# Attention scores by half blocks of 160 columns, six transfers a head pair, and the product with the global values by 64 rows

## The chip, the cores and the metric

The program runs on one core of one Trainium2 chip. The metric is the device time of one execution in microseconds. Before the change it is 891.88 us, the median of 3 runs (891.61 to 892.87).

## The reference

Attention feeds two feed-forward layers. There are 4 batches of 8 heads, 512 local tokens, 32 global tokens and 64 values a head. A global token looks at all 544 keys; a local one looks at the 32 global keys and at the local keys at most 32 places away.

```python
s_g = scale * np.matmul(q_g, k_all.transpose(0, 1, 3, 2))      # 32 x 544
out_g = np.matmul(sm(s_g), v_all)
mask = np.abs(pos[:, None] - pos[None, :]) <= 32
s_ll = np.where(mask, scale * np.matmul(q_l, k_l.transpose(0, 1, 3, 2)), -1e9)
s_lg = scale * np.matmul(q_l, k_g.transpose(0, 1, 3, 2))
a_l = sm(np.concatenate([s_lg, s_ll], axis=-1))
out_l = np.matmul(a_l, np.concatenate([v_g, v_l], axis=2))
x = concatenate([out_g, out_l]) as 2176 tokens x 512
x = (silu(x @ w_gate) * (x @ w_val)) @ w_out                   # d_ff 1536
h = x @ w_in;  out = (h * tanh(softplus(h))) @ w_out           # d_ff 2048
```

All inputs are float32, the feed-forward weights float64.

## The kernel before, in words

**Two parts.** The first is attention (`attention`, L537) for 16 head pairs, n = 0 to 15, four to a batch. With it run the conversion of the first six weight tiles and, as filling, two tiles (512 and 384 tokens) of the first feed-forward group (`add_fill`, L640). The second part is the rest of both feed-forward layers, placed by a planner (`run`, L1323) that works from its own costs and due times and is untouched by the change.

**The order of the attention part** is written out: `ORDER` (L221) is a string with a letter for each task, `KINDS` (L218) says what each letter is and on which of its two possible engines it runs, and `in_order` (L242) walks it and hands out PSUM banks. There are two double banks, `PAIR`, and four single ones, `ONE`; a task that needs a bank takes the next free one and holds it until a named task has read it. Each engine works through its own tasks in that order, and so does SP's queue with its transfers. After the first 18 TensorE tasks `attention` puts in as many products of zeros (`keep_busy`, L155) as the digits of `steady` (L550) say, 19 in all, and `setup` puts in 7.

**A head pair** (`add_pair`, L265) goes through these tasks:

- `qk`, SP: `load_qk` (L172) has two transfers for k (L178) and four for q (L180 to L183), the last rows of q together with the first ones. For pair 0 the q transfers are on ACT's queue. `v`, SP: `load_v` (L195) has four, windows of 128 keys that start every 64 keys (L202 to L204).
- `A`, TensorE: 16 transposes of k and q by 64 rows (L212, tiles `ks`, `qs`) into a double bank. `Ak`, `Aq`, DVE or ACT: copies to SBUF (L237 or L235, `kst`, `qT`).
- `Ag`, `At`, POOL: the global keys and the overlapping 64 keys of the next block are copied into `kst` (L287, L293, L294), so that each of the four blocks of 128 queries has 192 local and 32 global keys side by side.
- `S`, TensorE (L314), one for each half g: for 2 blocks and 2 heads a product of 64 rows (a head's values) and 128 output lines (queries) with 224 columns, into a double bank, a head to a bank.
- `M`, DVE (L325): mask and row minimum of 224 columns, one instruction for each block and head. `E`, ACT (L332): exponential with its sum. `R`, DVE: reciprocal. `N`, POOL or DVE (L344, L346): product with the reciprocal, 4 x 192 and 4 x 32 columns.
- `C`, TensorE (L212, `sm`, `sng`): 10 transposes of the weights into a double bank. `V`: copied to SBUF (`pt`).
- `D`, TensorE (`values`, L374): first 8 products with the global values (L378; 128 rows, of which `vg` has zeros in all but 32, 64 output lines, 128 columns), then 16 with the local ones (L382; 128 rows, 64 output lines, 64 columns), all into one single bank. `Xc`: copied out; `Xh`, `Xl`: split into two parts; `Xd`: stored.

**The global queries** go two head pairs at a time (`add_glob`, L398): `GA` (L408) 2 products of 512 columns, `GM`, `GE`, `GR`, `GN` as above, `GT` 10 transposes (tile `sg`), `GO` (L454) 20 products of 32 columns. `add_batch` (L472) turns the global keys and queries (L478).

**Float32 products** are recorded as two instructions each, transposes as one: the 4 products of an `S` task show as 8.

Of the kernel before, what the change touches and what calls it, by code (L numbers as in the profile page):

```python
# [21 lines left out]
def tile_attn_moe_moe2(  # L22
# [57 lines left out]
    kst_p = pool("kst", 2, early)  # L80
# [11 lines left out]
    mask = e_p.tile([128, 224], F32, name="mask")  # L92
    mask7 = e_p.tile([128, 224], F32, name="mask7")
    qgbd = e_p.tile([128, HP, 2, SG], F32, name="qgbd")
    vg = e_p.tile([128, 4, HP, D], F32, name="vg")
    vgb = e_p.tile([128, H, D], F32, name="vgb")

    def setup():
        nc.gpsimd.memset(ident, 1.0)
        nc.gpsimd.affine_select(out=ident, in_=ident, pattern=[[-1, 128]], compare_op=ALU.is_equal,  # L100
                                fill=0.0, base=0, channel_multiplier=1)
        keep_busy(0, 7)
        nc.vector.memset(qgbd, 0.0)
        for t in (vg, vgb):
            nc.vector.memset(t, 0.0)

        nc.gpsimd.memset(mask, 0.0)
        m = mask[:, 0:192]
        nc.gpsimd.affine_select(out=m, in_=m, pattern=[[1, 192]], compare_op=ALU.is_ge,
                                fill=NEG, base=0, channel_multiplier=-1)  # L110
        nc.gpsimd.affine_select(out=m, in_=m, pattern=[[-1, 192]], compare_op=ALU.is_ge,
                                fill=NEG, base=64, channel_multiplier=1)

        nc.gpsimd.tensor_copy(mask7, mask)
        nc.gpsimd.memset(mask7[64:96, 128:192], NEG)
        nc.gpsimd.memset(mask7[96:128, 64:128], NEG)
# [4 lines left out]
    def x_copy(src, key, cols, name):  # L121
        XF[key] = sm_p.tile([128, 512], F32, tag="xf", name="xf")[:, 0:cols]
        duplicate(name, XF[key], src)
# [26 lines left out]
    QS, KS, VW, KST, GK = {}, {}, {}, {}, {}  # L150
# [21 lines left out]
    def load_qk(b, hp):  # L172
# [6 lines left out]
        for h in range(2):  # L179
            eng.dma_start(out=qs[:, 0:3, h],  # L180
                          in_=q_l[b, 2 * hp + h, SG:SG + 384, :].rearrange("(c p) d -> p c d", p=128))
        eng.dma_start(out=qs[0:96, 3], in_=q_l[b, hs, SG + 384:SL, :].rearrange("h p d -> p h d"))
        eng.dma_start(out=qs[96:128, 3], in_=q_l[b, hs, 0:SG, :].rearrange("h p d -> p h d"))  # L183
        QS[b, hp], KS[b, hp] = qs, ks

    def load_vg(b):

        for k in range(4):
            nc.sync.dma_start(out=vg[32 * k:32 * k + 32, k],
                              in_=v_g[b].rearrange("(g h) p d -> h p g d", h=2)[k % 2])  # L190

    def load_vgb(b):
        nc.sync.dma_start(out=vgb[96:128], in_=v_g[b].rearrange("h p d -> p h d"))

    def load_v(b, hp):  # L195

        hs = slice(2 * hp, 2 * hp + 2)
        vw = v_p.tile([128, NB, 2, D], F32, tag="vw", name="vw")
        for h in range(2):
            v = v_l[b, 2 * hp + h]  # L200
            windows = bass.AP(v.tensor, v.offset, [[D, 128], [64 * D, NB - 1], [1, D]])
            nc.sync.dma_start(out=vw[:, 0:NB - 1, h], in_=windows)  # L202
        nc.sync.dma_start(out=vw[0:64, NB - 1], in_=v_l[b, hs, SL - 64:SL, :].rearrange("h p d -> p h d"))
        nc.sync.dma_start(out=vw[64:128, NB - 1], in_=v_l[b, hs, 0:64, :].rearrange("h p d -> p h d"))  # L204
# [5 lines left out]
    def transpose_half(out, src, j):  # L210
# [7 lines left out]
    KINDS = ("qk A gk w Ak+1 Aq At Cq AG AGk Ag S M E AGe GG GA GGe+1 Cf GM R vg v vgb N Ak GE GR GN C V "  # L218
             "Ch GT GV D AGk+1 Aq+1 GO Xc GXc+1 Xd GV+1 Cl Xc+1 GXh+1 Xh Xh+1 Xl GXl V+1 Ch+1 GXd F_v "
             "F_g GXc Ft Fg Fp Fh Fl Fh+1 GXl+1 F2 Fy Fy+1 GXh Xl+1").split()  # L220
    ORDER = "abcdaefgchaijkllmkmmmmmmnnnnibopedcnqgnramsnntbskfelfhluvammmmmmmmwnxnnngyybizgsAnBCkfDEDEnqsslmmFnnGcHm"  # L221
    ORDER += "muwnntlbnIemnnJAyayKmmmigDEDoBslkCEalpLkmmmmmnMnnumnGnnnmNmnnnIyywOwPbaQRDznESfOqDlsuyETUlmmmmmmmmnnnnyI"
    ORDER += "DDnrnnEngVVkWdtLXbwAlMefIusYZcmvOlmmQmgnUnnBbmmmM01ayymzhsnnf2DDnEEnCdqlssscgVGwnIUHamnmlummMVtnSAnyWyk1"
    ORDER += "YmmmmnnnnnUb0zxKOZaDXQiiDBlEjhul3Immm4kCyg1mmmmmVb5nnnnnnnnDsLefyEGwuoRTHl6DqEpy2lmOnmnmymnSgsbekkrfImmm"
    ORDER += "nnmDZwOadaE7nWns1tsYcDlgLEQVlmmAmmbInnnnu3eRmmyyqkmmKlUnn2D0wvVRBnEtDC4mmm00USWgVncm5GnuEhnnlOwy1s8xiHbd"
    ORDER += "7msmmyAnIefaDnnsmEn13nBCilsnMDjou0LyyEmmmml4wOGnnnngphmmmZkPrIDmw5Dnnnn0uEEbUlYssImeOMOmmmfUn2SqskyyVaDD"
    ORDER += "sZaELgEtlFQQlMImnnVkmmmm9TAnmBmmbVCnM2nnn!!xzufnnn#ylb!y!emmnnnSm#n6Km#gkwvwDDXX17gnZlOOddulmm$UIqWyymmm"
    ORDER += "mmmtGD1nnnnnnnnEu0P3ADVl45EL6lwIwmmnmnnmnyyBmmm7mNZnnnnDCuD!My!OREyXUGI%DU9PDEL$#X&VI2%9OMTOMUZ!!$$O&&"
# [36 lines left out]
    def add_pair(n):  # L265
# [15 lines left out]
        def kst():  # L281
            if (b, hp) not in KST:
                KST[b, hp] = kst_p.tile([128, 4, 224], F32, tag="kst", name="kst")
            return KST[b, hp]

        def glob_keys():
            nc.gpsimd.tensor_copy(kst()[:, :, 192:224], GK[b, "kT"][:, hp:hp + 1, :].to_broadcast([128, 4, SG]))  # L287

        def keys():
            duplicate(("Ak", n), kst()[:, :, 0:128].rearrange("c r (j t) -> c r j t", j=2), R["pk"])  # L290

        def more_keys():
# [1148 lines left out]
```

## Time and profile before

| | us |
|---|---|
| median of 3 runs | 891.88 |
| the profiled execution | 890.72 |
| its span, first to last instruction | 889.0 |
| attention part, to the last of its products | 159.0 |
| TensorE busy | 877.6 |
| DVE, ACT, POOL busy | 649.6, 490.8, 541.3 |

The granted TensorE clock is at full speed throughout the span. Busy time counts every moment at which an instruction of the engine is under way, its tail included, so a TensorE that is busy isn't one that starts instructions as fast as it can. Transfers have no busy time of their own on the queue that issues them; the queue's timeline shows how long each issue takes.

### The profile page before, as it was taken

How to read it: one execution, taken by the hardware profiler on the slowest of the kernel's cores; microseconds unless marked ns; L12 is line 12 of the kernel's file. 1: busy time of each engine (PE TensorE's matmuls, PEld its weight loads, DVE VectorE, ACT ScalarE, POOL GpSimd, SP SyncE). 2: the span in 40 equal slices, each digit the busy share in tenths (PEclk: the TensorE clock that was granted, in tenths of full speed). 3: DMA queues.
4: the chain of work that ended last, by engine and by line, in shares of the span. 5: the costliest groups of instructions: out<-in, count | busy, mean ns of one | idle time of the engine just before them, and what ended most of it. 6: DMA issues, size and time to landing. Idle time of an engine off the chain costs nothing.

```text
span 889.0 us, 17205 instructions
## 1 busy us (share of the span) xinstructions
PE 877.6 (99%) x6252; PEld 808.0 (91%) x6252; DVE 649.6 (73%) x1224; ACT 490.8 (55%) x1177; POOL 541.3 (61%) x550
## 2 busy tenths in 40 slices
PE   7999999999999999999999999999999999999998
PEld 6777888988999999999999999998989898989896
DVE  5777786779777888778778899777777777753434
ACT  6888886454435454455455678764445444544341
POOL 4798887699964386375374799564454436633231
PEclk9999999999999999999999999999999999999999
DMA  7777775577555646646546335664737374726283
GB/s 167 169 182 168 189 173 147 197 233 240 195 190 197 224 148 209 205 139 230 178 153 221 137 142 194 224 222 156 250 116 261 121 263 139 259 80 197 61 266 144
DMA packets 165334, 164.19 MB, mean 185 GB/s; under 512 B 81793, under 2 KB 143745, under 8 KB 165249
## 3 DMA queue, kind: packets, MB, share of 16 engines
q1 hardware_dynamic: 163824, 162.24, 57.8%
q8 instruction: 49, 0.80, 0.4%
q10 hardware_dynamic: 1424, 0.85, 0.3%
q14 instruction: 37, 0.30, 0.1%
HBM read 136.31 MB, written 26.74 MB: 183 GB/s over the span
## 4 chain that ended last, share of the span: by engine, by line
PE 94%; DMA 2%; SPq 1%; DVE 1%; ACT 0%; issue 0%; ACTq 0%; DVEq 0%
PE p L1127 37%; PE p L1232 21%; PE p L1018 15%; PE p L1084 8%; PE one L650 3%; PE pair L212 2%; PE pair L314 2%; PE one L378 1%; PE one L382 1%; DMA qs<-in_q_l 1%; PE one L454 1%; DMA gkq<-in_q_g 1%; PE one L408 1%; DMA vw<-in_v_l 0%; SPq L178 0%
## 5 line engine op out<-in xcount | busy, mean ns | idle before, releaser
L1127 PE MATMUL p<-xh,w 128*128 128x384 f32 (+1 forms) x992 | 258.3, 326 | 0.0
L1232 PE MATMUL p<-w,a 128*128 128x512 f32 x816 | 194.3, 391 | 0.0
L1232 PEld LDWEIGHTS p<-w,a 128*128 128x128 f32 x816 | 152.2, 188 | 29.9
L1127 PEld LDWEIGHTS p<-xh,w 128*128 128x128 f32 x992 | 176.9, 188 | 1.4
L1127 PE MATMUL p<-xl,w 128*128 128x384 f32 (+1 forms) x496 | 161.5, 326 | 0.0
L1139 ACT ACTIVATE b<-p 128x384 f32<-128x384 f32 (+1 forms) x144 | 68.0, 472 | 158.1 <-PE p L1127 153.7
L1018 PE MATMUL p<-a,w 128*128 128x384 f32 (+2 forms) x768 | 142.8, 334 | 0.0
L1048 POOL TENSOR_TENSOR a<-b,a 128x384 fp32r<-128x384 f32 (+1 forms) x58 | 62.0, 1068 | 117.9 <-ACT a L1046 76.6
L1018 PEld LDWEIGHTS p<-a,w 128*128 128x128 f32 x768 | 130.5, 188 | 2.8
L1242 DVE TENSOR_TENSOR y<-p,y 128x512 f32<-128x512 f32 x119 | 82.1, 690 | 65.3 <-PE p L1232 63.8
L880 POOL TENSOR_TENSOR w<-cx,w 128x256 fp32r<-128x256 f32 (+1 forms) x90 | 100.0, 1119 | 44.4 <-ACT w L879 38.9
L833 DVE TENSOR_TENSOR b<-p,b 128x384 f32<-128x384 f32 (+1 forms) x144 | 76.3, 531 | 64.2 <-PE p L1127 42.9
L1048 POOL TENSOR_TENSOR a<-s,a 128x384 fp32r<-128x384 f32 (+2 forms) x53 | 61.5, 1161 | 65.8 <-ACT a L1046 65.8
L1127 PE MATMUL p<-e,w 128*128 128x384 f32 (+1 forms) x528 | 101.3, 328 | 0.0
L1127 PEld LDWEIGHTS p<-xl,w 128*128 128x128 f32 x496 | 93.1, 188 | 1.5
L1127 PEld LDWEIGHTS p<-e,w 128*128 128x128 f32 x528 | 90.0, 188 | 1.0
L1027 DVE TENSOR_TENSOR y<-p,y 128x384 f32<-128x384 f32 (+2 forms) x116 | 62.5, 542 | 22.7 <-PE p L1018 21.3
L1084 PE MATMUL p<-xh,w 128*128 128x384 f32 (+1 forms) x256 | 72.6, 355 | 0.0
L1046 ACT ACTIVATE a<-s 128x384 fp32r<-128x384 f32 (+2 forms) x88 | 45.4, 516 | 47.0 <-DVE s L1070 45.9
L591 DVE SCALAR_TENSOR_TENSOR fl<-q,st 128x512 f32<-128x512 f32 x68 | 62.4, 918 | 9.8 <-ACT q L583 9.6
L595 DVE SCALAR_TENSOR_TENSOR cx<-fl,cx 128x512 uint32<-128x512 uint32 x68 | 65.9, 969 | 0.5
L332 ACT ACTIVATE sm<-sm,nb 128x224 f32<-128x224 f32 x128 | 60.0, 473 | 3.7 <-DVE nb L325 3.6
(153 smaller groups left out, 1512.9 us busy)
## 6 DMA issues: line engine op xcount, KB each, us to landing
e<-td SPq DMA_DIRECT2D x76, 384.0 KB
xh<-td SPq DMA_DIRECT2D x38, 384.0 KB
xl<-td SPq DMA_DIRECT2D x38, 384.0 KB
st<-in_moe_w_out SPq DMA_DIRECT2D x28, 512.0 KB
st<-in_moe_w_in SPq DMA_DIRECT2D x16, 512.0 KB
vw<-in_v_l SPq DMA_DIRECT2D x32, 224.0 KB
e<-td SPq DMA_DIRECT2D x20, 320.0 KB
st<-in_moe_w_gate SPq DMA_DIRECT2D x12, 512.0 KB
```

The costliest lines, as they stand in the source:

```text
L591: nc.vector.scalar_tensor_tensor(fl, q, TINY2, hw, op0=ALU.is_ge, op1=ALU.mult)
L595: nc.vector.scalar_tensor_tensor(x, fu, 0xC0000000, x, op0=ALU.bitwise_and, op1=ALU.bitwise_or)
L833: return lambda e: vec(e).tensor_tensor(out=out(), in0=a(), in1=b(), op=op)
L880: add(lo or [("POOL", PO(n))], 0, lambda e: vec(e).tensor_tensor(out=dst(1), in0=src(), in1=dst(0).bitcast(F32), op=ALU.subtract), r=[rd, ...
L1018: nc.tensor.matmul(ps.h[:, 0:n], lhsT=a.h[:, d], rhs=b.h[:, at:at + n], start=(i == 0 and j == 0), stop=(i == len(ws) - 1 and j == 2))
L1027: add("DVE", DV(n), lambda e: nc.vector.tensor_tensor(out=ya, in0=ps.h[:, 0:n], in1=ya, op=ALU.add), r=[ps], w=yt)
L1048: t.append(add(either(n), 0, lambda e: vec(e).tensor_tensor(out=dst(1), in0=get(), in1=dst(0).bitcast(F32), op=ALU.subtract), r=[v, (av[0] ...
L1084: nc.tensor.matmul(ps.h[:, 0:n], lhsT=a.h[:, d], rhs=b[:, c, c0:c0 + n], start=(c == 0 and j == 0), stop=(c == KD - 1 and j == 2))
L1127: nc.tensor.matmul(ps.h[:, 0:n], lhsT=w.h[:, 256 * a + 128 * c:256 * a + 128 * c + 128], rhs=xs[b][:, c, :], start=(start and c == 0 and j ...
L1139: add("ACT", AC(n), lambda e: nc.scalar.activation(out=dst.h[:, 0:n], in_=src.h[:, 0:n], func=AF.Copy), r=[sv], w=[dst])
L1232: nc.tensor.matmul(ps.h, lhsT=a.h[:, d], rhs=b.h, start=(i == 0 and q == 0), stop=(i == len(ws) - 1 and q == 2))
L1242: add("DVE", DV(512), lambda e: nc.vector.tensor_tensor(out=ya, in0=pa(), in1=ya, op=ALU.add), r=[ps], w=tok)
```

## The change

Scores are computed by half blocks of 64 queries: each has 128 local keys (32 to either side), read straight from one stretch of turned keys with 32 zeros at either end (`KT`, two of them), and 32 global keys, read from the batch's turned global keys. So a block has 160 columns instead of 224, and the POOL tasks `Ag` and `At` and the tile `kst` are gone. The tokens are no longer rotated by 32, so q comes in 2 transfers and v in 1 for both heads (3 for the first and the last pair, where the windows would leave the tensor); the edge values that the global queries lack are loaded once a batch into `vgb`. In `D`, the global values of both heads stand side by side in 128 output lines, so that one product of 64 rows serves two heads; the two blocks of a half use the upper and the lower 64 rows and go to two PSUM banks, and `D` holds a double bank instead of a single one. The order string is new, with 16 digits of zero products (12 in all, and the 7 at the start as before). Output rows are written in one piece a batch.

```diff
+    mask = e_p.tile([128, 160], F32, name="mask")
+    mask0 = e_p.tile([128, 160], F32, name="mask0")
+    mask7 = e_p.tile([128, 160], F32, name="mask7")
+    KT = [e_p.tile([128, SG + SL + SG], F32, name=f"kt{i}") for i in range(2)]
+    SGT = e_p.tile([128, SG + S], F32, name="sgt")
-    vg = e_p.tile([128, 4, HP, D], F32, name="vg")
+    vg = e_p.tile([128, HP, 2, D], F32, name="vg")
...
         for h in range(2):
-            eng.dma_start(out=qs[:, 0:3, h],
-                          in_=q_l[b, 2 * hp + h, SG:SG + 384, :].rearrange("(c p) d -> p c d", p=128))
-        eng.dma_start(out=qs[0:96, 3], in_=q_l[b, hs, SG + 384:SL, :].rearrange("h p d -> p h d"))
-        eng.dma_start(out=qs[96:128, 3], in_=q_l[b, hs, 0:SG, :].rearrange("h p d -> p h d"))
+            eng.dma_start(out=qs[:, :, h], in_=q_l[b, 2 * hp + h].rearrange("(c p) d -> p c d", p=128))
...
     def load_vgb(b):
+        nc.sync.dma_start(out=vgb[64:96], in_=v_l[b, :, SL - SG:SL].rearrange("h p d -> p h d"))
         nc.sync.dma_start(out=vgb[96:128], in_=v_g[b].rearrange("h p d -> p h d"))
...
+        def windows(x0, x1, r0, r1):
+            at = v.offset + (64 * x0 - SG + r0) * D
+            nc.sync.dma_start(out=flat[r0:r1, x0:x1], in_=bass.AP(v.tensor, at, [[D, r1 - r0], [64 * D, x1 - x0], [1, D]]))
+        first, final = (b, hp) == (0, 0), (b, hp) == (B - 1, HP - 1)
+        windows(int(first), 2 * NB - int(final), 0, 128)
...
+    ORDER = "abcdefeaafghijhjkkkkkklkbkmmmenooooocdopjjakkkkhbooqroookikkkoostctuevvoowxowyzbxamAcrBvvCujjkkkkkpooook"
...
         def scores(g):
-            p = both(("S", n, g))
+            p, keys = both(("S", n, g)), KT[n % 2]
             for pp in range(2):
-                for h in range(2):
-                    nc.tensor.matmul(p[:, h, 224 * pp:224 * pp + 224], lhsT=R["qT"][half(h), 2 * g + pp, :],
-                                     rhs=KST[b, hp][half(h), 2 * g + pp, :], start=True, stop=True)
+                r = 2 * g + pp
+                for j in range(2):
+                    i = 2 * r + j
+                    for h in range(2):
+                        nc.tensor.matmul(p[half(j), h, 160 * pp:160 * pp + 128], lhsT=R["qT"][half(h), r, half(j)],
+                                         rhs=keys[half(h), 64 * i:64 * i + 128], start=True, stop=True)
+                    for h in range(2):
+                        nc.tensor.matmul(p[half(j), h, 160 * pp + 128:160 * pp + 160], lhsT=R["qT"][half(h), r, half(j)],
+                                         rhs=GK[b, "kT"][half(h), hp, :], start=True, stop=True)
...
-            task(("S", n, g), "PE", [("Aq", n), ("At", n), ("Ag", n)], lambda g=g: scores(g), 2, ("M", n, g, 3))
+            task(("S", n, g), "PE", [("Aq", n), ("Ak", n), ("AGk", b)], lambda g=g: scores(g), 2, ("M", n, g, 3))
...
         def values():
-            p, vw = one(("D", n)), VW[b, hp]
-            for r in range(4):
-                for h in range(2):
-                    nc.tensor.matmul(p[half(h), 128 * r:128 * r + 128], lhsT=vg[:, 2 * (r % 2) + h, hp, :],
-                                     rhs=R["pt", r // 2][:, :, 4, :], start=(r == 0), stop=False)
+            p, vw = both(("D", n)), VW[b, hp]
+            for g in range(2):
+                for pp in range(2):
+                    nc.tensor.matmul(p[:, pp, 128 * g:128 * g + 128], lhsT=vg[half(pp), hp].rearrange("k h d -> k (h d)"),
+                                     rhs=R["pt", g][half(pp), :, 4, :], start=(g == 0), stop=False)
             for i in range(NB):
                 for h in range(2):
-                    nc.tensor.matmul(p[half(h), 64 * i:64 * i + 64], lhsT=vw[:, i, h, :],
+                    c = 128 * (i // 4) + 64 * (i % 2)
+                    nc.tensor.matmul(p[half(h), i // 2 % 2, c:c + 64], lhsT=vw[:, h, i, :],
                                      rhs=R["pt", i // 4][:, i % 2, 2 * (i // 2 % 2) + h, :],
...
-        task(("D", n), "PE", [("V", n, 0), ("V", n, 1), ("v", n), ("vg", b)], values, 1, ("Xc", n))
+        task(("D", n), "PE", [("V", n, 0), ("V", n, 1), ("v", n), ("vg", b)], values, 2, ("Xc", n))
...
-        task(("AGk", b), "DVE ACT", [("AG", b, 0)] + prev(("Ag", HP * b - 1), ("GG", b - 1)), keys)
+        task(("AGk", b), "DVE ACT", [("AG", b, 0)] + ([("S", HP * (b - 1) - 1, 1), ("GG", b - 2)] if b > 1 else []), keys)
...
-        steady = iter("040202002030020013")
+        steady = iter("0300200002031001")
```

Up to the first `D`, TensorE's tasks by the old string are A0 AG S0 S0 AG A1 GG GA A2 S1 S1 A3 AG C0 C0 GA S2 GT S2 A4 D0, and by the new one A0 AG S0 AG S0 A1 GG GA S1 S1 AG A2 C0 C0 A3 S2 S2 GA D0. Up to the first v tile, SP's transfers are those of qk0 to qk4, w (twice), gk (three times), vg and v by the old string; by the new one qk4 comes behind v.

## Rows read from the trace of the kernel before

**Rows 1.** The page: span and part 1, busy us, share, instructions.

```profile
span 889.0 us, 17205 instructions
PE 877.6 (99%) x6252; PEld 808.0 (91%) x6252; DVE 649.6 (73%) x1224; ACT 490.8 (55%) x1177; POOL 541.3 (61%) x550
```

**Rows 2.** Stages: length, busy us and instructions by engine, clock, DMA share, GB/s.

```profile
0.00:27.10 27.10, 22.61 (x231) 17.50 (x231) 15.62 (x66) 18.86 (x57) 13.14 (x35) 1.00 0.74 171
27.10:51.60 24.50, 23.12 (x454) 19.52 (x452) 18.06 (x77) 21.81 (x73) 21.46 (x30) 1.00 0.72 169
51.60:159.00 107.40, 105.67 (x1591) 87.54 (x1591) 80.46 (x283) 84.52 (x270) 87.19 (x102) 1.00 0.69 171
159.00:889.00 730.00, 726.17 (x3984) 683.47 (x3982) 535.45 (x802) 365.62 (x777) 419.49 (x385) 1.00 0.56 188
```

**Rows 3.** A stage, products of zeros (L157) alone: PE, PEld.

```profile
0.00:27.10 27.10, 9.62 (x52) 7.94 (x52) 1.00 0.74 171
```

**Rows 4.** The chain that ended last: start us, us, what; PE's blocks.

```profile
25.71 0.96 PE pair L314 x8
26.67 0.49 PE pair L212 x16
...
114.21 0.64 PE pair L212 x16
114.85 0.81 PE pair L314 x8
...
120.53 1.71 PE pair L314 x16
122.25 1.02 PE one L378 x16
123.27 0.93 PE one L382 x32
...
143.10 1.29 PE one L454 x40
...
154.85 0.90 PE one L378 x16
```

**Rows 5.** The same chain at the start.

```profile
8.44 2.46 DMA gkq<-in_q_g
...
15.52 3.70 DMA qs<-in_q_l
...
19.35 0.51 PE pair L212 x8
...
27.16 1.02 PE one L378 x16
```

**Rows 6.** Timeline of SP's queue: start us, us, what, how many.

```profile
0.80 0.99 SPq L178 DMA_DIRECT2D ks<-in_k_l  x2
...
24.91 0.61 SPq L204 DMA_DIRECT2D vw<-in_v_l  x1
...
133.57 1.00 SPq L579 DMA_DIRECT2D st<-in_moe_w_gate  x2
```

**Rows 7.** Groups of instructions to 159 us: busy, mean ns, idle before.

```profile
L325 DVE CUSTOM_DVE_ANT_0 sm<-pair,mask 128x224 f32<-128x224 f32 x128 | 42.6, 385 | 21.4 <-PE pair L314 16.0 <-PE pair L212 1.7 <-POOL sng L346 1.7
L414 DVE TENSOR_REDUCE gmx<-one 128x1 f32<-128x512 f32 x8 | 5.4, 677 | 1.9 <-PE one L408 1.9
L332 ACT ACTIVATE sm<-sm,nb 128x224 f32<-128x224 f32 x128 | 60.0, 473 | 3.7 <-DVE nb L325 3.6
L421 ACT ACTIVATE sg<-one,grc 128x512 f32<-128x512 f32 x8 | 5.4, 681 | 0.0
L344 POOL TENSOR_TENSOR sm<-sm,rc 128x768 f32<-128x768 f32 x32 | 48.3, 1508 | 11.2 <-DVE rc L338 8.0 <-ACT xf L235 2.4 <-ACT pt L235 0.9
L346 POOL TENSOR_TENSOR sng<-sm,rc 128x128 f32<-128x128 f32 x32 | 14.2, 444 | 0.0
L293 POOL COPY kst<-kst 128x192 f32<-128x192 f32 x16 | 6.7, 419 | 10.6 <-ACT kst L235 9.6 <-DVE kst L237 1.0
```

**Rows 8.** The chain: two blocks of the global scores.

```profile
37.78 1.57 PE one L408 x4
...
137.92 0.86 PE one L408 x4
```

More of the change, by code (lines that the diff above doesn't have):

```diff
@@ L107, in setup, with x_copy @@
         nc.gpsimd.memset(mask, 0.0)
[L108 to L116, printed above, removed]
+        for j in range(2):
+            m = mask[half(j), 0:128]
+            nc.gpsimd.affine_select(out=m, in_=m, pattern=[[1, 128]], compare_op=ALU.is_ge,
+                                    fill=NEG, base=0, channel_multiplier=-1)
+            nc.gpsimd.affine_select(out=m, in_=m, pattern=[[-1, 128]], compare_op=ALU.is_ge,
+                                    fill=NEG, base=64, channel_multiplier=1)
+        for t in (mask0, mask7):
+            nc.gpsimd.tensor_copy(t, mask)
+        nc.gpsimd.memset(mask0[half(0), 0:SG], NEG)
+        nc.gpsimd.memset(mask7[half(1), 128 - SG:128], NEG)
+        for t in KT:
+            nc.gpsimd.memset(t[:, 0:SG], 0.0)
+            nc.gpsimd.memset(t[:, SG + SL:], 0.0)
+        nc.gpsimd.memset(SGT[:, 0:SG], 0.0)
     XF = {}
-    def x_copy(src, key, cols, name):
+    def x_copy(src, key, cols, name, split):
         XF[key] = sm_p.tile([128, 512], F32, tag="xf", name="xf")[:, 0:cols]
-        duplicate(name, XF[key], src)
+        duplicate(name, XF[key].rearrange("c (g k t) -> c g k t", **split), src)
     def gx_copy(src, key, name):
@@ L325, in minimum @@
             nc.vector.tensor_tensor_reduce(
-                out=R["sm"][:, x], in0=both(("S", n, g))[:, h, 224 * pp:224 * pp + 224],
-                in1=mask7 if 2 * g + pp == 3 else mask, scale=-scale, scalar=3.0e38,
+                out=R["sm"][:, x], in0=both(("S", n, g))[:, h, 160 * pp:160 * pp + 160],
+                in1=(mask0, mask, mask, mask7)[2 * g + pp], scale=-scale, scalar=3.0e38,
                 op0=ALU.add, op1=ALU.min, accum_out=R["nb"][:, x:x + 1])
@@ L354, in turn @@
                 for j in range(2):
[L355 removed]
+                    transpose_half(p[:, j, 64 * k:64 * k + 64], R["sm"][half(j), 4 * g + k, 0:128], j)
             for j in range(2):
@@ L407, in scores @@
                 lq = qgbd[:, 2 * up + e].rearrange("c h r -> c (h r)")
-                nc.tensor.matmul(one(("GA", u))[half(e)], lhsT=lq, rhs=KST[b, 2 * up + e][:, :, 0:128],
+                nc.tensor.matmul(one(("GA", u))[half(e)], lhsT=lq, rhs=KT[e][:, SG:SG + SL],
                                  start=True, stop=True)
@@ L418, in exponential @@
         def exponential():
-            sg = R["sg"] = g_p.tile([128, S], F32, tag="sg", name="sg")
+            sg = R["sg"] = SGT[:, SG:]
             R["su"] = GSUMS[u % 2]
@@ L710, in out_rows @@
     def out_rows(c0, n):
-        parts = [(b * SL + lo, hi - lo, b * S + r) for b in range(B)
-                 for lo, hi, r in ((0, SL - SG, 2 * SG), (SL - SG, SL, SG))]
-        parts += [(B * SL + b * SG, SG, b * S) for b in range(B)]
-        for at, k, r in parts:
-            a, e = max(c0, at), min(c0 + n, at + k)
-            if a < e:
-                yield a - c0, r + a - at, e - a
-    def out_rows(c0, n):
-        parts = [(b * SL + lo, hi - lo, b * S + r) for b in range(B)
-                 for lo, hi, r in ((0, SL - SG, 2 * SG), (SL - SG, SL, SG))]
+        parts = [(b * SL, SL, b * S + SG) for b in range(B)]
         parts += [(B * SL + b * SG, SG, b * S) for b in range(B)]
```

80 lines of the change are left out of this document (33 added, 47 removed).

## The prediction

> **What bounds the kernel now.** I read the page first, then the stages, the chain that ended last, the queue of SyncE (SP), and the groups of the other engines. On the page TensorE (PE) is busy for 877.6 of 889.0 us [rows 1]. The stages [rows 2] separate what this change can touch from what it can't: the last instruction of the attention part's products stands at 159 us, and from there to the end PE is busy 726.17 of 730.00 us with 802 DVE, 777 ACT and 385 POOL instructions that the change leaves as they are, in the same order. I forecast those 730 us unchanged: the whole effect is the moment at which the first stage ends. Within it two parts differ. Up to 27.1 us PE is busy 22.61 us, but 9.62 of these are products of zeros, fillers that the program puts where it expects a wait [rows 3]. From 27.1 to 159 us there are no fillers, and PE shows only 24.50 - 23.12 + 107.40 - 105.67 = 3.1 us of idle time: there PE is the bound, and every instruction that the change gives it or takes from it counts.
>
> The chain gives prices, since its pieces are start-to-start times without the overlapping tails [rows 4]. Eight instructions of a scores block (four products; each float32 product is recorded as two instructions) take 0.81 us behind transposes and 0.96 us behind a product of another shape; sixteen take 1.71, so eight more cost 0.75 us. Sixteen with the global values cost 1.02 or 0.90, thirty-two with the local ones 0.93, and forty small ones 1.29 us. Three pairs of rows (0.96 and 0.81, 0.64 and 0.49, 1.02 and 0.90) differ only in whether the block before used the same split of the array in rows and columns: a change of split costs 0.12 to 0.15 us.
>
> The start hangs on transfers: the chain runs from a 2.46 us landing of the global queries to a 3.70 us landing of a q tile, and PE turns that tile at 19.35 and comes to the first values product at 27.16 us [rows 5]. SP issues one transfer after another all the while: the first at 0.80, the 42nd (the last of the first v tile) at 24.91 us and done 0.61 later, and it is still at it without a pause at 133.57 us [rows 6]. That is 24.72 / 42 = 0.59 us an issue.
>
> **The change part by part**, sum against the profiled execution (890.72 us, span 889.0, so 1.7 us lie around it; it lies 1.2 us under the median of the three runs, 891.88).
>
> *Scores.* A block of one half of a head pair was 4 products of 224 columns, and is 16: eight of 128 and eight of 32 columns, each with 64 rows and 64 output lines. So 32 instructions in place of 8. Fewer columns are computed for each query, but PE pays by the instruction when they are this small: 0.93 us / 32 = 0.029 us, and 1.29 / 40 = 0.032 us, for columns of 64 and of 32 [rows 4]. With 0.029 a block is 0.93 us, 0.18 more than 0.75; 32 blocks: +5.8 us. No row shows products on quarters of the array. Bound below: the four quarters run side by side and no issue cost binds; one quarter then has two rounds of two 128-column steps (a step is two instructions, 0.90 / 8 = 0.113) and two 32-column steps (0.93 / 16 = 0.058), 0.68 us: -2.2 us. Bound above: the two column halves run one behind the other, four such rounds, 1.37 us: +19.8 us. I take +5.8, since the rows with 64 output lines show two halves of the columns already side by side, and the issue cost is measured on instructions of just these sizes.
>
> The Trainium skill (TensorE: Matmul & The Clock Gate, section on issue steps) gives a floor of about 25 ns from one start to the next however few the columns; by it a block would be 0.80 us and the 32 would cost +1.6 us. The rows have 29 ns at 64 columns and 32 ns at 32, so the rows decide.
>
> *Values with the global keys.* Before, eight products of 128 columns, one for each head and block pair, half of the rows of the stationary tile being zeros; after, four, with both heads side by side in 128 output lines and the two block pairs on the two row halves. Sixteen instructions become eight: 0.90 / 2 = 0.45 us less for each of 16 pairs, -7.2 us. Bound: nothing, if the two row halves don't overlap. I take all of it, since the scores rows show two row halves side by side (0.75 us for eight instructions of 224 columns).
>
> *Changes of split.* Counted over both order strings with their fillers, there are 106 before and 140 after: the scores leave the split that the transposes use, and the values product now has two splits within itself. 34 more by 0.15 us: +5.1 us. Bounds: nothing, where the drain falls into a wait, and 34 times 0.15.
>
> *The start.* A head pair took 11 transfers (k 2, q 4, v 4, x 1) and takes 6 (2, 2, 1, 1). What SP issues ahead of the first values product, in the new order, is 29 in place of 42 transfers (the fifth q and k tiles move behind it too): the last is issued at 0.80 + 29 x 0.59 = 17.9 us. The tile for the fourth transposes is complete with the 22nd issue, 13.8 us, plus 3.70 to land, 17.5 us; then PE has two scores blocks and a global block, some 3.5 us, and reaches the values product near 21.5 in place of 27.16 us. Of these 5.7 us the fifth transposes and the global turn, 1.1 us of work, only move behind it; I take -4.5 us. Bounds: nothing (the elementwise chain holds the start instead) and -6. The first q tile comes with two issues on ACT's queue in place of four; that is inside this term. The new order also puts the second global transpose ahead of the second scores block, so everything on PE would stand behind the global queries if they were late; SP issues them some 6 places sooner, which covers it.
>
> *Other engines.* The minimum on DVE (0.385 us), the exponential on ACT (0.473) and the normalising product on POOL (1.508) go from 224 columns to 160 and from 768 elements to 512, and three POOL copies a pair go (the largest has 419 ns) [rows 7]. At most in proportion (64/224) that is 128 x 0.11 = 14 us of DVE and 128 x 0.135 = 17 of ACT, and their rows of 512 columns (0.677 and 0.681) say half of that on DVE and a third on ACT; POOL loses 32 x 256 x (1508 - 444) / 640 ns = 14 us and the copies. None of it is on PE, so I cost it at nothing by itself: it shortens what PE waits for. After 27.1 us I let it, together with the lighter SP queue, take 3.2 us, the idle time seen plus a little that hides inside blocks (a global block of 0.86 us once shows 1.57 [rows 8]). Bounds: -4 to +6, the upper end from the bank below. Added set-up on POOL (half masks, zero edges) lies ahead of the first minimum, where POOL idles. The four added transfers of value edges and the added wait for the older batch's scores stand far ahead of their use: nothing.
>
> Sum: 5.8 - 7.2 + 5.1 - 4.5 - 3.2 = -4.0 us: 886.7 for the profiled execution, and with its 1.2 us to the median **887.9 us**.
>
> **The rivals.** *The column halves don't overlap* (slower). The place is the scores block, the price +19.8 in place of +5.8, so the sum is +10.0 and the median 901.9 us; at half the overlap it is +3 and 894.9. It decides from 0.31 us more a block, 1.06 us in all. For it: only two streams at once are seen in any row. Against it: both row halves and column halves do overlap, each alone. The Trainium skill (same page, The mechanism) says that products start and end strictly in program order; by that the second column half would begin only when the last product of the first has started, which is this rival. The rows don't decide it, as two streams in order look the same.
>
> *The waits move to the double bank* (no change). The values product and its copy now hold one of two double banks, which scores, transposes and turned blocks share, in place of one of four single ones: 104 holders in place of 88. If each waits 0.3 us longer for the copy (the copies there are 0.7 us long), 16 x 0.3 = 4.8 us: +0.8, 892.7 us. The same result comes if SP isn't what holds the start, so that the 4.5 us stay: 892.4 us. Against: SP's queue has no pause there.
>
> *More is gained.* If the drains fall into waits that stay (0 in place of 5.1) and the start gives its -6, the sum is -10.6: 881.3 us. For it: fillers fall from 26 products to 19, so waits at the start are still planned.
>
> **How the numbers follow.** What a measurement of this kernel can tell from no change is 0.2%, 1.8 us. My forecast, faster by 2 to 7 us, has 0.46; more gained 0.17; no change 0.15; slower by the column halves 0.22. So faster 0.63, same 0.15, slower 0.22. The range leaves out the far ends of the first and the last: 880 to 897 us; the likeliest case alone has 885 to 890.
>
> **What would show it.** Right: the attention part ends near 155 us; scores blocks of 32 instructions at 0.93 us plus 0.15; eight instructions with the global values at 0.45; the first values product near 21.5 us; SP with pauses long before 134 us; 730 us behind. Wrong: scores blocks of 1.1 us or more; PE idle in front of transposes or values with the releaser a copy out of a double bank; a first values product still past 25 us; or a last stage that isn't 730 us.

## The result, and the profile after

The changed kernel takes 883.76 us (median of 4 runs, 883.02 to 884.73) beside 892.01 (891.61 to 892.87, 4 runs) of the kernel before on the same chip: a ratio of 0.9907, interval 0.989 to 0.9924. It is 8.3 us faster. The forecast was 887.9 us, 4.0 less than the median it started from; so the sign and the range (880 to 897) held, and the gain was twice the forecast's.

The profiled execution took 884.73 us, 6.0 us less than the profiled one before (890.72); the medians lie further apart, since the one before lay 1.3 us under its median here and this one lies 1.0 us over its own. The page of the changed kernel, its span and part 1, answers to [rows 1]:

```profile
span 882.5 us, 18336 instructions
PE 871.0 (99%) x6878; PEld 803.0 (91%) x6878; DVE 643.0 (73%) x1244; ACT 480.2 (54%) x1164; POOL 507.8 (58%) x503
```

Its stages (columns as in [rows 2]):

```profile
0.00:23.70 23.70, 19.56 (x335) 15.39 (x335) 14.13 (x69) 15.93 (x56) 8.92 (x33) 1.00 0.84 192
23.70:51.60 27.90, 24.55 (x574) 21.05 (x573) 18.48 (x83) 22.19 (x78) 16.98 (x20) 0.94 0.88 206
51.60:152.77 101.17, 100.71 (x1991) 83.07 (x1991) 71.91 (x291) 76.90 (x257) 62.71 (x67) 1.00 0.72 167
152.77:882.50 729.73, 726.20 (x3984) 683.54 (x3983) 538.51 (x803) 365.15 (x777) 419.24 (x385) 1.00 0.56 188
```

The last stage has 729.73 us where it had 730.00: as forecast, the whole effect is when the attention part ends, at 152.77 instead of 159.0 us. In the last 101 us of it PE is idle for 0.46 us, where [rows 2] have 1.73. The share of the transfer engines up to 51.6 us has risen from 0.74 and 0.72 to 0.84 and 0.88. And in the second stage the clock is 0.94 in the mean: for about 3.4 us from 32.5 us on it is at the lower level, 1.2 GHz, soon after PE had waited for 1.2 us (29.53 in the chain below). At half speed that costs some 1.7 us of this execution; the three others show a mean clock of 1.000 and spans of 880.9 to 881.8 us.

The chain of the changed kernel (start us, us, what): the start as in [rows 5], then a values product and scores blocks as in [rows 4]:

```profile
4.36 4.85 DMA gkq<-in_q_g
...
12.27 4.05 DMA gkq<-in_k_g
...
23.71 0.65 PE pair L384 x8
...
29.53 1.20 issue
30.73 1.36 PE one L461 x39
...
82.30 0.50 PE pair L384 x8
82.80 1.08 PE pair L389 x32
83.88 0.39 PE pair L317 x8
84.26 0.09 PE pair L320 x6
84.36 0.24 PE pair L317 x7
84.60 0.10 PE pair L320 x5
84.70 0.33 PE pair L317 x7
...
91.65 0.24 PE pair L317 x7
...
92.32 1.58 PE one L657 x6
```

The first values product (L384) stands at 23.71 us, between the 27.16 of before and the 21.5 forecast. A scores block (from 83.88 to 84.70) is two rounds of 128-column (L317) and 32-column (L320) products. Behind a change of split it takes 0.82 us; one that follows another, from 91.65 to 92.32, takes 0.67 (the one from 84.70 on took 0.77), where [rows 4] give 0.75 and the forecast said 0.93.

The timeline of SP's queue (start us, us, what) now has pauses, where [rows 6] had none: from 63.75 to 67.22 us, for instance.

```profile
62.68 1.07 SPq L583 DMA_DIRECT2D st<-in_moe_w_out  x1
67.22 2.31 SPq L209 DMA_DIRECT2D vw<-in_v_l  x2
```

### The profile page after: what moved, and what is told of

Its sections match the earlier page's. It is cut to its first block, busy times and chain, and to the rows that moved or that the text cites. A ratio compares the mean times of both kernels' runs of the same rounds, so it can differ in the third digit from the quotient of the medians.

```text
span 882.5 us, 18336 instructions
## 1 busy us (share of the span) xinstructions
PE 871.0 (99%) x6878; PEld 803.0 (91%) x6878; DVE 643.0 (73%) x1244; ACT 480.2 (54%) x1164; POOL 507.8 (58%) x503
## 4 chain that ended last, share of the span: by engine, by line
PE 97%; DMA 1%; issue 1%; ACT 0%; SPq 0%; DVE 0%; ACTq 0%; DVEq 0%
PE p L1122 38%; PE p L1227 21%; PE p L1013 15%; PE p L1079 8%; PE one L657 4%; PE pair L226 3%; PE pair L389 2%; PE pair L317 2%; PE one L461 1%; PE pair L384 1%; PE one L415 1%; PE pair L320 1%; DMA gkq<-in_q_g 1%; DMA gkq<-in_k_g 0%; SPq L177 0%
## 5 line engine op out<-in xcount | busy, mean ns | idle before, releaser
L602 DVE SCALAR_TENSOR_TENSOR cx<-fl,cx 128x512 uint32<-128x512 uint32 x68 | 63.0, 926 | 0.6
L604 DVE SCALAR_TENSOR_TENSOR cx<-st,cx 128x512 uint32<-128x512 uint32 x68 | 61.6, 908 | 0.4
```

Source lines behind the costliest of these rows:

```text
L602: nc.vector.scalar_tensor_tensor(x, fu, 0xC0000000, x, op0=ALU.bitwise_and, op1=ALU.bitwise_or)
```

## The experiments: which part carries the gain

**Scores and transfers apart.** The parts were put into the kernel before one at a time, with its order of the work. The transfers alone:

```diff
-            eng.dma_start(out=qs[:, 0:3, h], in_=q_l[b, 2 * hp + h, SG:SG + 384, :]...)
-        eng.dma_start(out=qs[0:96, 3], ...)
-        eng.dma_start(out=qs[96:128, 3], ...)
+            eng.dma_start(out=qs[:, :, h], in_=q_l[b, 2 * hp + h].rearrange("(c p) d -> p c d", p=128))
...
+        windows(int(first), 2 * NB - int(final), 0, 128)
```

> The kernel before with the six transfers of the change for its eleven and nothing else: its wide score blocks, its order and its product with the global values by 128 rows stay. The query and value rows are then not turned as its key windows want them, so the outputs are other numbers; the instructions and their sizes are those of before. Theory (the transfers carry most of the gain, since putting eleven back cost 13.7 us): about 886.5 us, 5.5 below before, first values product before 24.5 us. Rival (eleven are dear only in the new order, the scores carry the gain): 891 us or more, within 1 us of before.

Measured: 885.60 us, ratio 0.9928 (0.9907 to 0.9949), beside 892.25: the theory for the time, though not its detail, since the first values product stays at 26.93 us.

The narrow scores alone, with the data cut into eleven transfers again:

> The kernel before with the narrow score blocks alone: its order of the work, its product with the global values by 128 rows in one bank, and eleven transfers a pair. Theory (the parts add up: 0.67 us a block for 0.75, 32 blocks): 889.4 us, 2.6 below before. Rival A (the scores carry the gain on their own): 886 us or less. Rival B (eleven transfers cost 13.7 us whatever the order, as beside the change's other parts): about 897.5 us.

Measured: 893.01 us, ratio 1.0011 (0.9999 to 1.0024): nothing gained, and none of the three expectations. This run doesn't price the scores by themselves, though. In its profiled execution the first values product comes at 30.83 us, 3.7 later than before, with the clock at its lower level for 6.8 us ahead of it, and the attention part ends at 160.97, 2.0 later; so behind its start it is 1.7 us shorter. Both together, on the old order and with the old product with the global values:

```diff
-    ORDER = "abcdefeaafghijhjkkkkkklkbkmmm..."
+    ORDER = "abcdaefchaijllmmmmmmmnnnnibop..."
...
-                    nc.tensor.matmul(p[:, pp, 128 * g:128 * g + 128], lhsT=vg[half(pp), hp]...)
+                    nc.tensor.matmul(p[half(h), 256 * g + 128 * pp:256 * g + 128 * pp + 128], lhsT=vg[:, 2 * pp + h, hp, :], ...)
```

> The changed kernel with the old order string (without its two POOL copy tasks) and its 19 zero products, and the old values product in one single bank, which that string needs; new scores and new transfers stay. Theory (the order itself is worth little): as with the old values product alone, +4 us, 888 us. Rival (the new order, which puts the fifth q and k tiles behind the first v tile and the fillers elsewhere, made the gain at the start): 890 us or more.

Measured: 883.87 us, 0.9919 (0.9903 to 0.9935), the time of the whole change within the intervals, and neither of the two expectations. So this is how the parts stand, as ratios to the kernel before:

| old order, old product | eleven transfers | six transfers |
|---|---|---|
| wide scores | 1 | 0.9928 |
| narrow scores | 1.0011 | 0.9919 |

Six transfers give 0.7%, 6.4 us, and narrow scores nothing that these runs can tell from zero, with six transfers or with eleven. Where the 6.4 us come from is read in the kernel with the transfers alone, whose instructions and order are those of before. The timeline of its products with the global values (start us, us), the first and the eighth:

```profile
26.93 1.09 PE L384 MATMUL one<-pt,vg 128*64 128x128 f32 x16
...
84.18 1.09 PE L384 MATMUL one<-pt,vg 128*64 128x128 f32 x16
```

The same view of the kernel before, for the eighth:

```profile
88.98 1.09 PE L378 MATMUL one<-pt,vg 128*64 128x128 f32 x16
```

The first is only 0.2 us earlier (27.09 in that view); the eighth 4.8; and the attention part ends at 154.16 instead of 159.0 us, 4.8 earlier still. So the transfers alone hardly move the first values product. They take waits out of the stretch from 27 to 89 us. The chain of the kernel before says which: it runs through three landings there,

```profile
42.18 3.75 DMA vw<-in_v_l
...
62.28 4.38 DMA gkq<-in_q_g
...
84.91 3.50 DMA qs<-in_q_l
```

of which the last two stand behind issues of SP that follow each other closely. The chain of the kernel with the transfers alone has no transfer in it from 20 to 154 us. The lead over the kernel before grows at these places: 1.6 us at 46, 3.5 at 69, 4.8 at 89 us of the latter's time. The stages of the kernel with the transfers alone show it in PE's idle time, 0.50 us from 27 to 51.6 and 0.19 behind, where [rows 2] have 1.38 and 1.73; the rest lies between instructions whose tails count as busy. The other 1.6 of the 6.4 us aren't in these two traces; the executions of this kernel have mean clocks of 0.999 and 1.000, those of the kernel before beside them 0.996 to 1.000.

```profile
27.00:51.60 24.60, 24.10 (x459) 20.51 (x460) 19.66 (x84) 23.01 (x79) 22.03 (x30) 1.00 0.86 197
51.60:154.16 102.56, 102.37 (x1583) 85.67 (x1582) 80.55 (x274) 82.99 (x265) 86.17 (x102) 1.00 0.70 170
```

**Eleven transfers in the changed kernel**, the same bytes:

```diff
-            eng.dma_start(out=qs[:, :, h], ...)
+            for c in (slice(0, 3), slice(3, 4)):
+                eng.dma_start(out=qs[:, c, h], ...)
...
+        cuts = (int(first), NB - 1, NB, 2 * NB - 1, 2 * NB - int(final))
+        for x0, x1 in zip(cuts, cuts[1:]): ...
```

> The changed kernel with q in 4 transfers and v in 4 for each pair, the same bytes in the same packets. Theory (SP's issues held the start): the first values product moves back from 23.7 us by 8 or more issues of 0.59, to about 27 us, and the time grows by 3 to 4 us, 887 us. Rival (the landing of the data holds the start, not its issue, and behind the start PE is the bound): under 1 us.

Measured: 897.49 us (896.13 to 899.37), ratio 1.0076 (1.0059 to 1.0093): 13.7 us over the changed kernel, slower than the kernel before, and far more than either expectation. Its first values product is back at 27 us, as the theory said, so the new order alone doesn't move it either:

```profile
27.01 0.72 PE L388 MATMUL pair<-pt,vg 64*128 64x128 f32 x8
```

About half of the 13.7 us can be put down to the clock. Its stages, with 20 to 25 and 48 to 59 us cut out (the clock is the third number from the end):

```profile
20.00:25.00 5.00, 5.00 (x78) 4.36 (x78) 3.73 (x13) 4.43 (x13) 1.66 (x2) 0.66 0.48 109
25.00:48.00 23.00, 18.26 (x432) 14.53 (x431) 14.53 (x73) 17.71 (x63) 13.68 (x16) 1.00 0.78 186
48.00:59.00 11.00, 10.43 (x175) 9.60 (x176) 5.26 (x25) 5.87 (x24) 4.41 (x5) 0.53 0.60 141
```

Between them PE is idle for 4.74 of 23 us; up to 60 us the list of waits has 4.0 us for the global keys and 1.3 for local values. Both times the clock falls to its lower level after PE has waited. A mean of 0.66 over 5 us is 3.4 us at half speed (2 x 0.34 x 5), and 0.53 over 11 us is 10.3; if the work done in that time would have taken half of it at full speed, 6.8 us are lost (1.7 in the changed kernel's own profiled execution). That the rest is the waits themselves is argued from these lists, not shown by a run.

**Is it SP's time, or the landing in more pieces?** Five transfers more a pair, of one row that nothing reads:

```diff
+            eng.dma_start(out=extra_t[k:k + 1, :], in_=k_l[0, 0, k:k + 1, :])
...
+            extra(eng, 1)
...
+        extra(nc.sync, 3)
```

> The changed kernel with five more transfers a head pair, of one row of 256 bytes each into rows of a tile that nothing reads: one behind each query transfer, three behind the values. The data and its six transfers stay as the change has them. Theory (what eleven transfers cost is SP's time to issue them, 80 more at about 0.59 us): near the 897.5 us of the run with the data cut into eleven, 893 to 900 us, first values product later than 29 us. Rival (it is the landing of data in more pieces that costs): within 2 us of the change, 882 to 886 us.

Measured: 895.45 us (891.86 to 898.36, 10 runs), ratio 1.003 (1.0013 to 1.0048). The data and its transfers are those of the change, and the time is 2.0 us under the run with the data cut into eleven. So it is the issuing of more transfers that costs, and not the cutting of the data: the theory, though not its detail, since the first values product came at 26 and not behind 29 us. Two stages of this kernel in which the clock was at its lower level for a part (3.4 and 6.9 us, worked out as above; another 3.4 us follow at 121 us, so that here too up to 6.8 us are the clock's):

```profile
18.00:22.00 4.00, 4.00 (x46) 3.37 (x44) 3.56 (x14) 2.52 (x8) 0.47 (x3) 0.57 0.62 142
...
45.00:53.00 8.00, 8.00 (x152) 7.40 (x154) 4.06 (x23) 5.77 (x22) 4.42 (x5) 0.57 0.71 164
```

The first three of its list of PE's waits up to 60 us (who waits for what, us in total, times, longest):

```profile
PE one L494 <- DMA gkq<-in_k_g: 2.5, 2, 2.2
PE pair L235 <- DVE xf L260: 1.6, 1, 1.6
PE one L494 <- DMA gkq<-in_q_g: 1.3, 1, 1.3
```

The second of these waits in the chain, and ahead of it SP's timeline:

```profile
35.90 3.06 SPq L185 DMA_DIRECT2D extra<-in_k_l  x3
...
39.51 0.50 SPq L147 DMA_DIRECT2D xf<-xf  x1
```

```profile
39.51 4.62 DMA xf<-xf
...
44.22 0.70 DVE xf L260
...
44.97 0.53 PE pair L235 x10
```

This is a path that the prediction did not have. SP comes to the store of an attention output (`Xd`, L147) at 39.51 us, behind three of the small transfers; the copy of a later values product (`Xc`, L260) waits until that buffer is out, at 44.22; and the copy holds the PSUM banks that the next transposes on PE need.

## The experiments: scores, values, order

**Scores by 128 lines.** Four products of 224 columns and 128 output lines a block, as before, all of them with local keys; everything else as in the change:

```diff
-                r = 2 * g + pp
...
+                for h in range(2):
+                    nc.tensor.matmul(p[:, h, 224 * pp:224 * pp + 224], lhsT=R["qT"][half(h), 2 * g + pp, :],
+                                     rhs=keys[half(h), 128 * (2 * g + pp):128 * (2 * g + pp) + 224], ...)
```

> The changed kernel with its scores computed as before, 4 products of 224 columns with 128 output lines a block, everything else as changed; the scores are then not the ones wanted, the time is. Theory (the quarters of the array run side by side, a block costs 0.67 us in place of 0.75): 32 x 0.08 = +2.6 us of products and 18 changes of split less at 0.15, -2.7: no change, within 1 us of 883.8. Rival, the price of the prediction (0.93 us a block, 0.029 us an instruction): 32 x 0.18 + 2.7 = 8.5 us faster, 875.3 us.

Measured: 882.21 us, ratio 0.99 (0.9885 to 0.9915), 1.5 us under the change by the medians and the same as the change within the intervals: near the theory, far from the rival. At the forecast's price this kernel would have gained some 8.5 us (32 x 0.18, and 18 changes of split fewer at 0.15: the trace counts 123 for 141). It is the block's price in the forecast that falls.

**Quarter by quarter.** In the change the products of a block go round the four quarters of the array; here all products of one quarter come first, then those of the next:

```diff
-            for pp in range(2):
-                r = 2 * g + pp
-                for j in range(2):
+            for j in range(2):
+                for h in range(2):
+                    for r in (2 * g, 2 * g + 1):
...
```

> The changed kernel with each score block issued quarter by quarter: all four products of one quarter of the array, then those of the next. Theory (TensorE starts a product on a free quarter whatever stands ahead of it in the block): 0.67 us a block still, 883.8 us, within 1.5 of the change. Rival (a product starts only after those ahead of it in the program): the four quarters one after another, four times 0.67 us a block, 2.0 us more for each of 32, about 948 us. Between the two: a look-ahead of a few products, some tenths of a us a block, 890 to 910 us.

Measured: 911.09 us (910.97 to 912.6), ratio 1.0218: 27.3 us more, 0.85 us a block, so some 1.5 us in all: between theory and rival, just above the range given for that. The chain of this kernel within a block:

```profile
105.85 0.27 PE pair L316 x4
106.12 0.09 PE pair L318 x4
106.21 0.27 PE pair L316 x4
```

Every 0.36 us four recorded instructions with 128 columns start: two products, on two quarters. In the change eight start together (L317 x8 in the timeline below), on four. So the quarters do run side by side, but only as far as the order of the program lets their products come up close together: the second product for a quarter that is still at work holds up the next quarter, here for one round.

The timeline of the changed kernel for one block (start us, us, how many):

```profile
83.81 0.46 PE L317 MATMUL pair<-kt,qT 64*64 64x128 f32 x8
84.08 0.28 PE L320 MATMUL pair<-gkT,qT 64*64 64x32 f32 x8
84.16 0.45 PE L317 MATMUL pair<-kt,qT 64*64 64x128 f32 x8
84.41 0.29 PE L320 MATMUL pair<-gkT,qT 64*64 64x32 f32 x8
```

The program gives four with 128 columns (the two row halves, first column half), four with 32, and then the second column half. The trace has eight and eight: the second half's 128-column products start ahead of the first half's 32-column ones that stand before them. The rule quoted in the prediction (the Trainium skill, TensorE: Matmul & The Clock Gate, The mechanism: products start and end strictly in program order) is therefore not borne out across quarters here; the run by quarters shows that the order still matters within a few products.

**Wider rows on VectorE and ScalarE**, to see whether their relief was worth anything:

```diff
-                out=R["sm"][:, x], in0=both(("S", n, g))[:, h, 160 * pp:160 * pp + 160],
+                out=R["sm"][:, x, o:o + 208], in0=both(("S", n, g))[:, h, 112 * pp:112 * pp + 208],
```

> The changed kernel with VectorE's minimum and ScalarE's exponential over 208 columns of a block instead of 160, 48 more, of which nothing is used; TensorE's products stay. From 385 and 319 ns (minimum over 224 and 160) it adds some 50 ns to each of 128, 6.4 us of VectorE, and some 40 ns to each of 128 on ScalarE, 5.2 us. Theory (part of the gain of the narrow blocks is that relief, on a path of TensorE to VectorE to ScalarE): 1.5 to 4 us more than the change, 885.3 to 887.8 us. Rival (both engines have room): within 1 us of the change.

Measured: 883.07 us (881.93 to 883.81), ratio 0.9895: no dearer than the change, the rival. The groups show that the cost was there, 369 and 459 ns in this kernel (the first two lines) beside 319 and 419 in the change (the last two):

```profile
L338 DVE CUSTOM_DVE_ANT_0 sm<-pair,wide 128x208 f32<-128x208 f32 x128 | 40.5, 369 | 12.0 <-PE pair L325 9.9 <-ACT sm L346 1.3 <-PE pair L231 0.4
...
L346 ACT ACTIVATE sm<-sm,nb 128x208 f32<-128x208 f32 x128 | 58.4, 459 | 5.0 <-DVE nb L338 4.8
...
L331 DVE CUSTOM_DVE_ANT_0 sm<-pair,mask 128x160 f32<-128x160 f32 x128 | 34.1, 319 | 14.2 <-PE pair L320 11.6 <-ACT sm L338 1.6 <-PE pair L226 0.8
...
L338 ACT ACTIVATE sm<-sm,nb 128x160 f32<-128x160 f32 x128 | 53.2, 419 | 5.1 <-DVE nb L331 5.0
```

6.4 us more of VectorE and 5.1 of ScalarE cost nothing at the end. No run gives POOL its old work back.

**The product with the global values** put back to 128 rows, sixteen instructions, the new order and the double bank kept:

```diff
-                    nc.tensor.matmul(p[:, pp, 128 * g:128 * g + 128], lhsT=vg[half(pp), hp]..., rhs=R["pt", g][half(pp), :, 4, :], ...)
+                    for h in range(2):
+                        nc.tensor.matmul(p[half(h), pp, 128 * g:128 * g + 128], lhsT=vg[:, 2 * pp + h, hp, :],
+                                         rhs=R["pt", g][:, :, 4, :], start=(g == 0), stop=False)
```

> The changed kernel with its product with the global values put back to 128 rows and one head at a time (16 instructions in place of 8, still in two banks). Theory (PE's own instructions set the end of the attention part): 16 x 0.40 us more of products, 16 changes of split less at 0.15 us, so +4.0 us over the changed kernel, 887.8 us. Rival (waits on other engines and transfers set it, and swallow what PE saves): under 1 us of difference.

Measured: 885.36 us, 0.9934 (0.9919 to 0.9949), 1.6 us over the change by the medians and 2.4 by the ratios, between theory and rival; the intervals overlap, so that this run alone excludes neither. PE's work went up by the 4.0 us expected (1.02 or 0.90 us for 0.65 or 0.50, and 0.93 for 1.08, in 16 pairs); about half of it reached the end. With the old order as well (above) it was none by the medians, 1.1 us by the ratios: the new order starts earlier and loses it again. The stages of the kernel on the old order show PE idle for 0.51 us from 27 to 51.6 us; in the changed kernel it is idle for 3.35 from 23.7 to 51.6.

```profile
27.00:51.60 24.60, 24.09 (x611) 21.27 (x608) 17.23 (x84) 22.10 (x80) 18.34 (x23) 1.00 0.83 194
```

**Three tries at the start.** The second scores block ahead of the second global transpose, which PE waits for at 7.6 us:

```diff
-    ORDER = "abcdefeaafghijhjkkk..."
+    ORDER = "abcdefeaafghijjhkkk..."
```

> The changed kernel with the first pair's second score block ahead of the second turn of the global rows in the order. TensorE waits 1.4 us there for the global queries to land, with the scores behind. Theory (at the start the landing of transfers sets the end): 882.5 us, 0.8 to 1.5 below the change, first values product at 22.5 to 23 us. Rival (VectorE's minimum chain or the next landing takes the wait over): 883.8 us, within 0.5 of the change.

Measured: 884.09 us (881.79 to 884.23), ratio 0.9912 (0.9887 to 0.9937): the same as the change, and so is its first values product, at 23.6 us. Its profiled execution has the clock at full speed throughout and a span of 879.6 us, 2.9 under the change's; two of the other three have a mean clock of 0.996. Next, also the last global value rows earlier, which PE probably waited for at 29.5 us:

```diff
-    ORDER = "...stctuevvoowxowyzbxam..."
+    ORDER = "...stctuzevvoowxowybxam..."
```

> The changed kernel with the first pair's second score block ahead of the second turn of the global rows, and the two transfers of the last global value rows ahead of the second batch's global queries, so that they are issued about 2 us earlier; TensorE waited 1.2 us for them at 29.5 us, after which the clock was at half for 3.4 us in the profiled execution. Theory (the landing of transfers sets the end up to some 40 us, and a wait there can cost the clock as well): 881.5 us, 2 below the change. Rival (the next landing takes the wait over, or the clock falls elsewhere): 883.8 us, within 1 of the change.

Measured: 883.92 us (882.29 to 886.44), ratio 0.9909 (0.9892 to 0.9925): the same again. And those rows, six transfers, issued by ScalarE's queue:

```diff
-            nc.sync.dma_start(out=vg[32 * k:32 * k + 32, :, k % 2], ...)
+            (nc.sync if b else nc.scalar).dma_start(out=vg[32 * k:32 * k + 32, :, k % 2], ...)
```

> The changed kernel with the second score block ahead of the second turn of the global rows, the last global value rows earlier, and the first batch's six transfers of global and edge value rows issued by ScalarE's queue instead of SP's: six of the some 31 issues that SP makes up to 23 us, about 3.5 us of its time. Theory (SP's issues still set the start): the local values and the second batch's global queries land earlier, 1 to 2 us below the change, about 882 us, first values product at 22.5 us or earlier. Rival (at 20 us the transfers themselves are the bound, their share of the 16 engines is over 0.9 there): 883.8 us, within 1 of the change.

Measured: 891.25 us (889.3 to 894.0), ratio 0.999 (0.9979 to 1.0002): 7.5 us worse than the change. ScalarE's timeline says why:

```profile
20.62 1.95 ACTq L194 DMA_DIRECT2D vg<-in_v_g  x2
22.68 0.60 ACT L249 ACTIVATE kt<-pair 128x512 f32<-128x512 f32 x1 [3.90 <-DMA vg<-in_v_g]
```

The third of the four issues had to wait, and ScalarE with it: 3.9 us, with a copy of keys and everything behind it on the engine. In the chain of this kernel what ended the wait is the landing of a v tile, issued by SP:

```profile
15.37 5.24 DMA vw<-in_v_l
20.62 0.32 ACTq L194
```

Why an issue on one queue waits for a landing of the other isn't shown. The first values product went to 32.8 us, and the mean clock to 0.990 to 0.996 in all twelve executions; in the profiled one the clock is at its lower level for 13.6 us up to 33 us, which by the working above is up to 6.8 of the 7.5 us. The Trainium skill (DMA: Bandwidth & Descriptors, Issuing engines are not separate DMA queues) says that a second issuing engine saves only the sequencer's time, "which is usually small relative to the DMA itself". Here that time matters, as the five small transfers show, and taking it from an engine with work of its own cost more than it gave.

## Why the prediction was right, and wrong

**Right.** The last stage is unchanged, all of it lies in when attention ends, and within the attention part SP's queue held work up. A change of split costs what the rows said: 0.82 for 0.67 us in a scores block. The number of changes up to the end of attention is 141 in place of 107, the 34 more of the forecast. That the column halves overlap settles the slower rival: 0.67 us a block, and not 1.06 or more.

**The step that failed is the price of the scores block.** The forecast took +5.8 us from 29 ns an instruction, a price of products on column halves, and kept -2.2 as the bound for four quarters side by side and no issue cost. The trace has that bound: 0.67 us, 32 x (0.67 - 0.75) = -2.6 us. This one step is off by 8.4 us, as much as the whole gain. The rows it stood on said so in part: a step of two instructions takes 0.113 us at 128 columns and 0.058 at 64, half, so the 29 ns at 64 columns still followed the columns and weren't a price by the instruction; and no row showed what an instruction costs on four quarters, 21 ns here. With their changes of split (18 in the new order, 19 in the old, +2.7 to +2.9) the scores are worth about nothing on PE, and three pairs of runs with and without them say so: by the ratios -0.8 us beside six transfers, +1.0 beside eleven and +0.6 in the changed kernel, none of it clear of the noise.

**That all of PE's work reaches the end is the second step that failed.** The values product was forecast at -7.2 and its inner changes of split at 2.4 of the 5.1. The blocks have -0.40 instead of -0.45 us (from 0.90 to 0.50), so the size was right: -6.4. But of the 4.0 us net, 1.6 to 2.4 came through, and 0 to 1.1 together with the order.

**The start and the later waits** were set at -4.5 and -3.2, the second partly for lighter VectorE, ScalarE and POOL. The first values product moved by 3.45 us with the new order and six transfers, by 0.2 with the transfers alone, and not at all with the new order and eleven; so it takes both to move it. SP's issues hold more than that product: the wide rows show that VectorE and ScalarE contribute nothing, and the transfers alone take 4.8 us out of 27 to 89 us. By the medians they are worth 6.4 us, where the two terms together said 7.7. The prediction looked for idle time of PE and found 3.1 us; time also hides in instructions with long tails, and in executions whose clock falls after a wait. The kernel before shows a mean clock of 0.995 to 1.000 in the executions beside these runs, its profiled one being among those at 1.000; that cost wasn't in the trace from which the forecast was made.

Put together by the ratios: transfers -6.4, narrow scores beside them -0.8, new order with the new product -1.1 (0 by the medians); the change has -8.3. The runs were made on different chips, and only the first of these parts is clear of the noise. For the same three the forecast had -7.7, +8.5 (the scores with 18 changes of split) and -4.8. So it was too dear by 9.3 us in the scores, and too hopeful by 3.7 to 4.8 in the values product and by 1.3 in the transfers. That the sum still had the sign, and lay within its range, is in part luck: the errors had opposite signs.

**Open.** Why the new order loses between 24 and 52 us what it wins before is not settled. PE is idle there for 3.35 us, and the clock costs 1.7 more in the profiled execution. The share of the transfer engines (0.88) suggests that the transfers themselves are the bound once their issue isn't; but of PE's waits only the one at 29.53 (1.2 us) may be for a transfer, and the others listed, 2.3 us in all, are mostly for copies on ScalarE and VectorE. The last try was to tell and showed something else. Nor was a version found that is measurably faster than the change: the two tries that changed only the order have its time.

## What to carry to other kernels

Count a queue's issues as an engine's work: 80 transfers of 256 bytes, which nobody read, cost more than all that the change gained: by late loads, by a late store that held a buffer, and by the clock behind these waits. A wait on TensorE can have a second price, the clock after it, so compare the mean clock of several executions before a term is drawn from one profile. And when a kernel is divided into smaller products, send them round the parts of the array: the same 32 instructions took 0.67 or some 1.5 us a block by their order alone.

## What was not expected of the hardware

- Products on four quarters start within 34 ns of one another (83.806 to 83.840 us in the trace, for the first four of the eight at 83.81), and 32 instructions take 0.67 us, 21 ns each, less than the 29 and 32 ns that [rows 4] give on halves.
- A 128-column product started ahead of 32-column ones that stand before it in the program; issued quarter by quarter only two quarters were at work at a time (0.36 us a round).
- After waits of PE the granted clock fell to 1.2 GHz for 3.4 us, or for 7 to 10 us, in the profiled executions of the change, of the runs with more transfers and of three others; with eleven transfers and narrow scores every execution showed it (mean clock 0.990 to 0.996), with six and wide scores none by more than 0.001.
- An issue on ScalarE's queue that had to wait held ScalarE for 3.9 us.
